# One order of pieces replaced by another in a fused Nyström attention and feed-forward kernel

## The chip, the core and the metric

The kernel runs on one core of a Trainium2 chip. The metric is the device time of one execution in microseconds (us). Before the change three runs took 248.09, 248.97 and 251.36 us, so the median is 248.97 us.

## The reference

Each of 8 batches has 8 heads, 576 positions and 64 columns a head. Queries and keys are averaged over 18 positions into 32 landmarks; three softmax matrices, an iterated inverse of the small one and the values give the attention's output, which goes through two dense layers with x * sigmoid(x) between them.

```python
q_lm = q.reshape(B, H, 32, 18, D).mean(axis=3)     # k_lm likewise
A  = sm(q, k_lm); Bm = sm(q_lm, k_lm); C = sm(q_lm, k)
Z  = Bm.T / (norm1(Bm) * norminf(Bm) + 1e-06)
for _ in range(6):
    Z = 2 * Z - Z @ Bm @ Z
x = A @ Z @ C @ v                                  # 4608 x 512
h = x @ w_in                                       # 512 x 2048
out = (h / (1 + exp(-h))) @ w_out                  # 2048 x 512
```

## The kernel before

The work is cut into some 1,500 named pieces. A piece is an object with a name, an engine, the pieces that it needs and a function that writes its instructions. The string SEQUENCE lists all names in one order; `Plan.run` walks it, gives each piece its PSUM banks (seven, and an eighth, bank 7, from the first piece of the second layer on) and its engine (`/ACT` or `/DVE` behind a name overrides the first choice), and the kernel writes the instructions in that order. Each engine then works through its own part of the list, in order, with semaphores where a piece needs another's data or buffer. No scheduler moves anything afterwards. A word `*n` stands for n fillers: matmuls of zeros into bank 7 that only keep TensorE busy.

Names used below, with the batch behind the dot and t = 1 for k, t = 0 for q, g for the half of the heads:

- `ld1.b`, `ld0.b`: load of k and q (GpSimd's queue, 576 KB each); `ldv0.b` to `ldv2.b`: the three loads of v (192 KB each); `wi..` and `wo..`: loads of the two weight matrices.
- `xt{t}{g}.b` (L539): DMA transpose of one half of k or q from the loaded tile `qk` to `qT`, issued on SyncE's queue, for batches 3 to 7. Batches 0 to 2 do this with TensorE pieces `tr..` and copies `trc..`.
- `lra`, `lrb`, `lrc`, `lrd{t}.b` (L575, VectorE): the sum over positions that makes the landmarks from `qT`; `ltr{t}.b` (TensorE) and `lmT{t}.b`: their transpose and its copy.
- `A.b`, `C.b`, `Ax..`, `Cx..`: the two large score matrices and their exponentials; `ct0.b`, `ct1.b` (L814): DMA transposes of the second one, on SyncE's queue, from batch 2 on; `cv.b`: the product with v.
- `ns..`, `nsd..`, `fb..`: the iterated inverse; `zt.b`, `m0.b` to `m3.b`: the product with the first weight matrix, two banks each, and their copies `mc{f}{g}.b` by ACT or VectorE.
- `h0.b` to `h15.b`, `hx0.b`, `hx8.b` (TensorE) and `g..`, `gx..` (ACT, L913 and L936): first layer and its activation; `h4` to `h7` read what `mc10` and `mc11` copied.
- `ss..@` (VectorE, L1001), `p1@` to `p7@` (TensorE) and `c..@`: the second layer as seven products of a block scheme; `os..@` (L978): four stores to the output, on SyncE's or ACT's queue.

Transfers wait for each other by hand. A piece's list `after` becomes a semaphore wait (L1126). Before the change it is fixed in code: `xt` of batch b and `ct` of batch b - 1 wait for `ldv1.b` (L534, L816), and the loads of batch b wait for the third transpose in the list of batch b - 1, which is `xt00`, and for `ct0` of batch b - 2 (L1096 to L1102). The list orders the transposes as xt10, xt11, xt00, xt01; SEQUENCE can issue them in another order.

## Time and profile before

| What | us |
|---|---|
| median of three runs | 248.97 |
| span of the profiled execution, first to last instruction | 245.4 |
| TensorE (PE) busy | 233.3 |
| ACT busy | 180.8 |
| VectorE (DVE) busy | 180.0 |
| weight loads (PEld), which overlap PE | 165.8 |
| GpSimd (POOL) busy, nearly all of it issuing loads | 36.7 |

The profile is of one execution. TensorE is busy in 95% of the span, in order, so the time is the sum of its pieces plus the waits between them. SyncE and GpSimd issue transfers; their rows show the issue, and a transfer lands later.

### The profile page before, as it was taken

The page shows a single profiled execution, that of the slowest core. Times are in us where ns is not written, and L with a number is a line of the kernel's source. Part 1 is how long each engine was busy: PE and PEld are TensorE (multiplying, and loading weights), DVE is VectorE, ACT ScalarE, POOL GpSimd, SP SyncE. Part 2 cuts the span into 40 slices and gives each one's busy share as a digit, 9 for nine tenths or more (in the row PEclk, how much of TensorE's full clock was granted, in tenths as well). Part 3 has the DMA queues.
Part 4 walks back from the last instruction along what each step waited for, and adds up shares of the span by engine and source line. Part 5 has one row for each costly group of instructions (what it writes and reads, how often), then busy time and mean ns, then how long its engine had stood idle before and what let it go on. Part 6 is the DMA issues. An engine that isn't in the chain of part 4 may idle for free.

```text
span 245.4 us, 7471 instructions
## 1 busy us (share of the span) xinstructions
PE 233.3 (95%) x2948; PEld 165.8 (68%) x2948; DVE 180.0 (73%) x503; ACT 180.8 (74%) x432; POOL 36.7 (15%) x62
## 2 busy tenths in 40 slices
PE   7999999999999999199999999999999999999992
PEld 5986464457867556067878754777876765789882
DVE  2589889789998591489798968938899475348752
ACT  3299999988989998159746699999779788634100
POOL 8346713000050040000130060000000000000000
PEclk9999999999999999769999999999999999999999
DMA  6999999999999999793999999985414421012343
GB/s 160 207 203 197 206 207 206 210 205 204 132 177 220 202 137 178 185 194 98 136 190 171 167 185 239 190 145 136 108 47 117 121 52 39 1 43 77 88 119 109
DMA packets 55876, 36.84 MB, mean 150 GB/s; under 512 B 36640, under 2 KB 47392, under 8 KB 55840
## 3 DMA queue, kind: packets, MB, share of 16 engines
q0 software_dynamic: 15120, 18.06, 45.1%
q1 hardware_dynamic: 39808, 17.35, 34.9%
q10 hardware_dynamic: 912, 0.95, 1.4%
q8 instruction: 23, 0.38, 0.6%
q14 instruction: 13, 0.11, 0.1%
HBM read 36.70 MB, written 9.44 MB: 188 GB/s over the span
## 4 chain that ended last, share of the span: by engine, by line
PE 78%; ACT 7%; DMA 7%; SPq 3%; issue 1%; DVE 1%; ACTq 0%; DVEq 0%
PE ps L325 74%; DMA qT<-qk 6%; PE ps L515 3%; SPq L539 2%; ACT gm L913 2%; DMA gm<-in_k_dram 1%; ACT L913 1%; SPq L814 1%; ACT L1116 1%; ACT gx L936 1%; ACT m L335 1%; PE ps L802 1%; DVE red L575 1%; ACT pb L641 1%; ACT et L742 0%
## 5 line engine op out<-in xcount | busy, mean ns | idle before, releaser
L913 ACT ACTIVATE gm<-ps 128x512 f16<-128x512 f32 x128 | 68.7, 621 | 15.0 <-PE ps L325 14.3
L325 PE MATMUL ps<-etn,m 128*128 128x512 bf16 (+1 forms) x512 | 73.5, 289 | 0.2
L325 PEld LDWEIGHTS <-gm 128*128 128x128 f16 x512 | 48.6, 98 | 12.5 <-issue 1.3
L325 PE MATMUL ps<-w_out_sb,gm 128*128 128x256 f16 (+1 forms) x392 | 53.0, 281 | 0.0
L325 PEld LDWEIGHTS <-ss 128*128 128x128 f16 x408 | 39.5, 99 | 9.8 <-issue 1.8
L325 PEld LDWEIGHTS <-m 128*128 128x128 bf16 x512 | 31.5, 98 | 20.8 <-issue 3.2
L325 PE MATMUL ps<-wt,ss 128*128 128x256 f16 x272 | 35.5, 276 | 0.2
L1036 DVE TENSOR_TENSOR ost<-ost,ps 128x256 f32<-128x256 f32 x51 | 20.9, 416 | 13.4 <-PE ps L325 7.4
L335 ACT COPY ost<-ps 128x256 f32<-128x256 f32 (+1 forms) x45 | 17.2, 388 | 10.9 <-PE ps L325 10.6
L335 ACT CAST m<-ps 128x512 bf16<-128x512 f32 x36 | 19.4, 612 | 1.1 <-PE ps L325 0.8
L337 DVE CAST m<-ps 128x512 bf16<-128x512 f32 x28 | 18.3, 685 | 2.3 <-PE ps L325 1.9
L710 DVE SCALAR_TENSOR_TENSOR st<-st,ps 128x128 bf16<-128x128 bf16 (+2 forms) x54 | 13.6, 257 | 8.5 <-PE ps L325 5.5
L407 POOL DMA_DIRECT2D v<-in_v_dram x24 | 14.0, 590 | 30.8 <-DMA qT<-qk 13.6
L325 PE MATMUL ps<-w_out_sb,ss 128*128 128x256 f16 x136 | 17.5, 273 | 0.0
L325 PE MATMUL ps<-wt,gm 128*128 128x256 f16 x120 | 15.5, 272 | 0.0
L575 DVE TENSOR_TENSOR red<-qT 128x1024 f16<-128x1024 bf16 x12 | 8.3, 689 | 9.4 <-DMA qT<-qk 9.2
L685 DVE TENSOR_TENSOR fb<-st,hmask 128x256 bf16<-128x256 bf16 (+1 forms) x54 | 14.4, 271 | 0.8
L752 ACT ACTIVATE ln<-ps 128x288 f32<-128x288 f32 x32 | 12.4, 423 | 2.7 <-PE ps L325 2.4
L787 ACT ACTIVATE ce<-ps 128x288 bf16<-128x288 f32 x32 | 13.0, 424 | 1.7 <-PE ps L325 1.6
L1001 DVE TENSOR_TENSOR ss<-gm 128x1024 f16<-128x1024 f16 x15 | 10.2, 686 | 5.2 <-ACT gm L913 5.2
L742 ACT ACTIVATE et<-ps 128x288 bf16<-128x288 f32 x32 | 11.1, 423 | 3.6 <-PE ps L325 3.6
L337 DVE COPY ost<-ps 128x256 f32<-128x256 f32 x25 | 10.5, 420 | 3.2 <-PE ps L325 3.0
(93 smaller groups left out, 332.0 us busy)
## 6 DMA issues: line engine op xcount, KB each, us to landing
out_dram<-ost SPq DMA_DIRECT2D x126, 64.0 KB, 2.1
v<-in_v_dram POOLq DMA_DIRECT2D x24, 192.0 KB, 10.0
qk<-in_q_dram POOLq DMA_DIRECT2D x7, 576.0 KB, 10.6
qk<-in_k_dram POOLq DMA_DIRECT2D x7, 576.0 KB, 9.2
w_out_sb<-in_moe_w_out_dram POOLq DMA_DIRECT2D x4, 512.0 KB, 15.1
w_in_sb<-in_moe_w_in_dram POOLq DMA_DIRECT2D x8, 128.0 KB, 7.2
w_in_sb<-in_moe_w_in_dram POOLq DMA_DIRECT2D x4, 256.0 KB, 9.0
out_dram<-ost ACTq DMA_DIRECT2D x10, 64.0 KB, 1.7
```

What stands on the lines that cost most here:

```text
L325: nc.tensor.matmul(out=out_ap, lhsT=lhsT, rhs=rhs, start=start, stop=stop, skip_group_check=True)
L335: nc.scalar.copy(out=out, in_=in_)
L337: nc.vector.tensor_copy(out=out, in_=in_)
L407: lambda e, a=a: nc.gpsimd.dma_start(out=v_r[b % 2][a * L:(a + 1) * L, :, :], in_=v[b].rearrange("h (l a x) d -> a l h (x d)", l=L, a=VA)[ ...
L575: lambda e: nc.vector.tensor_tensor(out=o_, in0=a_, in1=b_, op=OP.add),
L685: nc.vector.tensor_tensor(out=fb[it % 2][:, g0:g1], in0=bc(sr[it % 3][:, g0:g1, 0:L], 4, 2), in1=bc(hmask, n, 1), op=OP.mult), [o], 14.5 + ...
L710: nc.vector.scalar_tensor_tensor(out=s2[:, g0:g1, lo:SW], in0=s[:, g0:g1, lo:SW], scalar=2.0, in1=ps[:, 0:NG * SW].rearrange("p (g x) -> p ...
L742: lambda e, g=g, et=et, c=c: nc.scalar.activation(out=et[:, c], in_=bank(me["A"], 2 * g + c)[:, 0:HS], func=AF.Exp, scale=sc / J),
L752: lambda e, g=g, c=c, ln=ln: nc.scalar.activation(out=ln[:, c], in_=bank(me["S", g, c])[:, 0:HS], func=AF.Ln),
L787: nc.scalar.activation(out=ce[:, :, 0:VP].rearrange("p (i c) (a l) -> p c a i l", c=2, a=VA)[:, c], in_=bank(me["C"], 2 * g + c)[:, 0:HS]. ...
L913: lambda e, dc=dc, cell=cell: nc.scalar.activation(out=gm[:, dc, :], in_=bank(cell["o"]), func=AF.Silu),
L1036: nc.vector.tensor_tensor(out=out_, in0=x, in1=y, op=OP.add)
```

## The change

SEQUENCE is replaced as a whole: the same pieces, the same 2,948 matmuls and the same 64 fillers stand in another order. Of the copies and evacuations 86 go to the other of ACT and VectorE (43 each way), and 13 of the last stores to the other queue. Fillers also stand behind the point from which bank 7 is used by other pieces; before, all of them stood ahead of it. The waits in `after` are no longer made in code but written behind the name: `ldv1.5<xt00.4<ct0.3` waits for both. They follow the same rule as before (`xt` and `ct` wait for `ldv1`, loads for `xt00` and `ct0`), but each piece's place in the order is new. The helper that kept the list of GpSimd loads goes.

```diff
@@ Plan.run @@
+        placed = {}
...
+            word, *gates = word.split("<")
             name, _, e = word.partition("/")
             o = named.pop(name)
-            assert all(id(d) in seen for d, _ in o.deps), name
-            seen.add(id(o))
+            placed[name] = o
+            o.after = [placed[x] for x in gates]
@@ load @@
-    swdge = []
-    def load(name, prio, us, issue, emit, deps=(), after=()):
-        d = list(deps) + list(after)
-        if len(swdge) >= 8:
-            d.append((swdge[-8], None))
-        o = A(name, [("POOL", issue)], emit, d, prio, dma=us)
-        o.after = after
-        swdge.append(o)
-        return o
+    def load(name, prio, us, issue, emit, deps=(), after=()):
+        return A(name, [("POOL", issue)], emit, deps, prio, dma=us)
@@ attn @@
-                    qt_ops[t, g][0].after = gate
-                ct_ops[g][0].after = v_ops.get(b + 1, [])[-2:-1]
```

The order around the transposes of batch 4, by queue, taken from the two sequences:

```
SyncE before:  ct1.3 ct0.3 xt00.4 xt11.4 xt01.4 xt10.4 os@5020.0 os@5021.0 xt11.5 ...
SyncE after:   xt10.4 os@5021.0 ct0.3 os@5101.0 ct1.3 xt01.4 xt00.4 os@5020.0 xt11.4 xt11.5 ...
GpSimd before: ld1.4 ldv1.4 ld0.4 ldv0.3 ldv2.3 ldv2.4 | ld1.5 ldv0.4 ldv1.5 ld0.5 | ld0.6 ...
GpSimd after:  ld1.4 ldv2.3 ldv2.4 ldv1.4 ldv0.3 ld0.4 | ldv1.5 ld1.5 ldv0.4 ld0.5 ldv0.5 | ld1.6 ...
DVE before:    mc01.3 mc31.3 mc10.3 mc11.3 ss00@5200 ss00@5220 ss10@5200 lra1.4 lrb1.4 lrc1.4 ss10@5220 ss20@5220 lrd1.4
DVE after:     mc01.3 mc21.3 mc30.3 lra1.4 ss00@5200 ss20@5200 mc11.3 ss10@5200 lrb1.4 lrc1.4 lrd1.4
PE after:      m0.3 m2.3 m3.3 h6.2 h3.3 m1.3 h0.3 h13.3 *1 h15.3 h12.3 h8.3 p1@5200 h2.3 h10.3 h6.3 ... p6@5200 h11.3 ltr1.4
```

The bar in GpSimd's rows stands where the next load waits for transposes (`<xt00.4<ct0.3` for the second group).

The order of the weight loads is new too:

```
GpSimd before, behind ld1.1: ldv2.0 ldv0.0 wi0b1 ldv1.0 wi0b0 wi1a wi0a wi1b1 wi1b0 wi3b0 wi3a wi3b1 wi2b0 wi2b1 wi2a ldv0.1 ldv1.1
GpSimd after, behind ld1.1:  ldv1.0 ldv0.0 wi0a wi1b0 wi0b0 ldv2.0 wi3b1 wi1a wi1b1 wi3a wi3b0 wi0b1 wi2b1 wi2a wi2b0 ldv2.1 ldv0.1 ldv1.1
```

## The prediction

> **What bounds it now.** The page first: TensorE is busy nearly all the time, and one slice is not.

> ```profile
> PE 233.3 (95%) x2948; PEld 165.8 (68%) x2948; DVE 180.0 (73%) x503; ACT 180.8 (74%) x432; POOL 36.7 (15%) x62
> ...
> PE   7999999999999999199999999999999999999992
> ...
> PEclk9999999999999999769999999999999999999999
> ```

> The busy row has a single 1, near 100 us, and right behind it the granted clock falls to 7 and 6 tenths. The waits of TensorE say what that is, and the busy time by stretch what it costs.

> ```profile
> engine line waited for: us in total, times, longest us
> PE ps L325 <- DVE rs L575: 5.4, 1, 5.4
> PE ps L325 <- DVE zer L434: 1.1, 1, 1.1
> PE ps L325 <- ACT qk L335: 0.5, 1, 0.5
> PE ps L325 <- DMA ct<-ce: 0.2, 1, 0.2
> ```

> ```profile
> 95.00:98.75 3.75, 3.75 (x40) 2.66 (x37) 0.00 (x0) 3.75 (x9) 0.00 (x0) 1.00 1.21 199
> 98.75:104.17 5.42, 0.00 (x1) 0.00 (x1) 2.83 (x7) 0.44 (x1) 0.00 (x0) 0.76 0.74 182
> 104.17:110.00 5.83, 5.83 (x29) 3.54 (x30) 4.74 (x12) 2.75 (x7) 0.00 (x0) 0.64 1.04 197
> ```

> One wait of 5.42 us, then 5.83 us of matmuls at a clock of 0.64: they lose 5.83 x 0.36 = 2.1. So 7.5 us hang on one event. Everything else that TensorE waits for over 0.15 us is 1.8 us, 1.6 of it at the start. The chain of waits between 76 and 106 us, in start, length, what, and GpSimd's timeline show the event:

> ```profile
> 80.56 3.22 SPq L539
> ...
> 83.89 1.30 SPq L539
> ...
> 85.28 1.39 SPq L539
> ...
> 86.72 14.41 DMA qT<-qk
> ...
> 101.23 0.70 DVE red L575
> ```

> ```profile
> 86.34 0.71 POOL L400 DMA_DIRECT2D qk<-in_k_dram  x1 [13.68 <-issue]
> 87.04 1.16 POOL L407 DMA_DIRECT2D v<-in_v_dram  x2
> 88.20 0.71 POOL L400 DMA_DIRECT2D qk<-in_q_dram  x1
> ```

> The four transposes of batch 4 are issued as xt00, xt11, xt01, xt10. The loads of batch 5 wait for xt00 alone, the first: it lands at 85.81, and ld1.5 goes out at 86.34. xt01.4, issued 1.06 us ahead of that (85.28), lands in 3.8 us, as undisturbed ones do (3.3 to 4.2 for eight others). xt10.4, issued 0.38 behind it, takes 14.4: it lands at 101.14, the last of the four loads at 100.90. VectorE stands at lra1.4 meanwhile (8.0 us), and ltr1.4 on TensorE behind that. A transpose of qT is 1,152 packets of 256 bytes in the trace, a load of k or q 256 packets of 2,304, and while both are queued they take turns.

> [...]

> **The change, by part.** Durations below are of the trace, spacings from the starts of successive pieces on one engine (h 0.43, p 0.87, m 0.26, hx 0.47, ss 0.60, mc on VectorE 0.68, lra 0.69). TensorE's pieces are the same set, 222.2 us at these spacings, so only waits differ. Up to batch 3's first m both orders hold 80.3 us of pieces.

> *The transposes of batch 4.* SyncE now issues xt10, a store group, ct0.3, a store group, ct1.3, xt01, xt00, a store group, xt11; the loads wait for xt00, the third. The start is the landing of ldv1.4. ld1.4 keeps its place (66.9, landed 73.3); two v loads now stand ahead of ldv1.4, at 1.05 to 1.7 each, so it lands near 76.6 instead of 75.78. Then 1.38 (xt), 1.84 (four stores of 0.43 with gaps), 1.3 (ct), 1.84, 1.3, 1.38: xt00.4 goes out at T = 86.0 with gaps, and lands at T + 3.6. GpSimd needs another 0.55 after a landing (85.81 to 86.34, 66.33 to 66.90), so ldv1.5 goes out at T + 4.15 = 90.15. xt11.4 goes out behind xt00.4 and one store group, at T + 3.3 = 89.3: 0.85 ahead of the loads. Between the two rows, 1.06 ahead (clean) and 0.38 behind (held), it is nearer to clean: landing 92.9. Bounds of the lead: 0.4 (landing in 3.3, stores 0.3 slower) and 1.1.

> *What lra1.4 holds on VectorE.* Before, all four mc of batch 3 stood ahead of it; now lra1.4, ss00, ss20 and then mc11.3. mc11.3 is done 0.69 + 0.60 + 0.60 + 0.68 + 0.1 behind xt11.4's landing: 95.6. h6.3 reads it. From m0.3 to h6.3 stand four m, nine h, a p and a filler: 1.06 + 3.89 + 0.87 + 0.11 = 5.93, so without new waits h6.3 comes at 87.77 (batch 3's first m in the trace) + 5.93 = 93.7, with those below at 95.4. Wait: 0.2 (0 to 1.9). ltr1.4 stands 5.7 us of pieces behind h6.3 and its sums are done 1.6 behind mc11.3, so the old wait does not come back there.

> *The weights.* wi0b1 moves from third to twelfth behind ld1.1. All twelve weight loads and three v loads land by 29.05 in the trace, in a DMA that is full (share 1.19 and 1.25 from 10 to 30 us); behind wi0b1 now stand wi2b1, wi2a, wi2b0 (0.45, 1.24, 0.7 in the trace's landings), so it lands at 26.6. m0.0 would be due at 24.8 (0.9 earlier in the list than its 25.7). It waits 1.9, of which later waits before the change (the pieces there fall back by 1.0 to 30 us) are saved again; cv.1, now 4.8 us of pieces earlier, waits for ldv1.1 at about 32.1 and adds 0.3. Net 1.2, bounds 0 and 2.

> *ct1.3.* It goes out at 83.2 instead of 77.8 and lands 2.5 later (the shortest; 4.4 the longest): 85.8. cv.3 is due at 84.9. Cost 0.8 (0 to 2.7); the wait for ct that cv.3 has now, 0.2 and 0.2 around it, goes.

> *Fillers behind the use of bank 7.* Each must wait for that bank's evacuation: h9.1, filler 1.3 us later, behind g9.1 on ACT, which takes 0.62 and has a table load of 1.28 ahead. No row shows a filler so placed. Bounds 0 and 1.4 for the three; I take 0.2, since most stand over an ACT queue that was not behind before.

> *Engines of copies.* 43 against 43; per kind 9 more c (0.42), 7 fewer trc (0.46) and 2 fewer mc (0.68) on VectorE: within 1 us of 180 either way, cost 0 unless one sits ahead of a waited-for piece. Dropping the GpSimd bookkeeping writes no instruction: 0. Tail: one evacuation and stores behind the last p, as now: 0, within 0.3.

> Sum against the profiled execution: 245.4 - 7.5 - 0.4 + 0.2 + 1.2 + 0.8 + 0.2 = 239.9. The median of the runs stands 3.6 above the span, so 243.5.

> **Rivals.**

> *xt11.4 is caught.* It decides at the lead: if xt11.4 goes out later than the loads do (stores ahead of it held by 0.9 us), it waits for five loads. Price: 14.4 as in the trace, 1.26 for a fifth load: landing 105.0, mc11.3 at 107.7, h6.3 12.1 late, and 2.1 for the clock. 239.9 + 14.2 = 254.1, a time of 257.7: slower. For it: SyncE's store groups were held for 9.57 us behind a caught transpose. Against it: at 86 us no load is in flight. Chance 0.19. If only two fifths of its packets are left, it is held for ldv1.5 and most of ld1.5, 3.8 us: up to 249.4 with the clock, the forecast's upper end.

> The row for the clock is one wait of 5.42 us with 2.1 lost behind it; no row has a wait between 1.1 and 5.4. [...]

> *Many small waits.* The old order left slack around most pieces; here h6.3, cv.3, m0.0 and fillers all stand within 1 us of what they need, so ACT's and VectorE's queues may do the same at ten other places of 0.3 to 0.6 us (the trace has some 7 us of small ones between pieces, by how far starts fall behind the sum of spacings). + 4.5: 248. Chance 0.16.

> *Nothing new is late.* 245.4 - 7.9 = 237.5: 241.1. For it: a piece's wait vanishes when its producer is 1 us earlier. Chance 0.10.

> **The numbers.** Forecast 243.5, chance 0.55, its own range 240.5 to 249.5. 2% is 5.0 us, about what a measurement can tell from no change: faster means below 244.0, slower above 253.9. Faster: 0.41 of the forecast's 0.55 and 0.10 = 0.51. Slower: 0.19 and 0.03 from small waits and a half-caught transpose = 0.22. Within: 0.27. Range 240 to 254: it leaves out most of the caught case (0.17) and 0.03 below.

> **What would show it.** Right: no slice of TensorE under 8 near 100 us and no fall of the clock; the wait for rs L575 gone; xt11.4 issued just ahead of ldv1.5 and landed in under 5 us; small waits for w_in's load near 26 us and for ct near 85. Wrong: a wait of several us at an h for VectorE near 95 us (caught), or TensorE's short gaps together 4 us over those of before.

## The result and the profile after

The changed kernel takes 255.96 us (median of 5 runs, 254.70 to 258.75), the kernel before, in the same measurement, 250.15 us (248.09 to 251.36). The ratio is 1.027, with an interval of 1.021 to 1.034: 2.7% slower where 243.5 us was forecast. The ratio leaves out the executions of both kernels that ran in a slower state, and the profiled one of the changed kernel is of these: its span is 256.9 us, those of the other four are 252.8 to 255.2. The same two rows of the page as before, with the busy line:

```profile
PE 238.0 (93%) x2948; PEld 167.0 (65%) x2948; DVE 179.8 (70%) x503; ACT 182.7 (71%) x432; POOL 36.8 (14%) x62
...
PE   8989999989999859999839999999999999999993
...
PEclk9999999999999968999988999999999999999999
```

The 1 near 100 us is gone. In its place stand a 5 near 93 us and a 3 near 131 us, each with a lower clock in it or behind it, and the first half has 8s where there were 9s. TensorE's waits name the two:

```profile
engine line waited for: us in total, times, longest us
PE ps L333 <- DMA ct<-ce: 8.3, 3, 4.9
PE ps L333 <- ACT gm L910: 1.6, 2, 1.1
```

For VectorE's rs 0.5 us are left of 5.4. 8.3 us are waits for `ct`, which were 0.2. By stretch (busy time of each engine, then granted clock, DMA share, GB/s):

```profile
88.70:93.10 4.40, 1.00 (x50) 0.63 (x50) 0.00 (x0) 1.83 (x4) 0.00 (x0) 0.85 0.56 131
93.10:99.20 6.10, 6.10 (x50) 3.41 (x54) 2.51 (x7) 3.17 (x6) 2.55 (x4) 0.55 0.92 174
99.20:127.60 28.40, 28.40 (x335) 20.75 (x335) 24.72 (x66) 22.53 (x58) 1.34 (x3) 1.00 0.91 155
127.60:132.90 5.30, 0.42 (x40) 0.24 (x24) 2.28 (x7) 0.14 (x1) 0.00 (x0) 0.99 0.99 202
132.90:138.00 5.10, 5.10 (x67) 3.37 (x59) 1.30 (x5) 2.25 (x9) 1.87 (x3) 0.68 0.76 114
```

Two stalls, each followed by 5 to 6 us at a clock of 0.55 to 0.68. Between them TensorE works through 99 to 127 us without a gap, which is where the old stall would have been. The second stall in SyncE's and GpSimd's timelines (start, length, what):

```profile
120.24 1.21 SPq L812 DMA_TRANSPOSE ct<-ce  x1
121.55 2.97 SPq L975 DMA_DIRECT2D out_dram<-ost  x4
124.63 1.21 SPq L812 DMA_TRANSPOSE ct<-ce  x1
```

```profile
124.37 0.71 POOL L399 DMA_DIRECT2D qk<-in_k_dram  x1 [24.54 <-DMA ct<-ce]
```

The loads of batch 6 wait for `ct0.4`, the transpose at 120.24. It lands, ld1.6 goes out at 124.37, and `ct1.4`, held behind a store group, follows 0.26 us later. It lands at 132.54, 7.9 us after its issue; in the kernel before it took 4.4, and 2.5 is the shortest. This is the event that the prediction described for `xt10.4`, with another transpose.

To set kernels side by side, the table uses the measure of the prediction: by how much the starts of TensorE's pieces fall behind the sum of their spacings, in us, over stretches of that sum (222.2 us in all). What it contains are waits and matmuls at a lower clock.

| kernel | 0-40 | 40-75 | 75-88 | 88-95 | 95-110 | 110-222 | all | span |
|---|---|---|---|---|---|---|---|---|
| before | 6.2 | 0.8 | 0.7 | 7.6 | 0.7 | 2.7 | 18.6 | 245.4 |
| changed | 9.4 | 2.9 | 6.8 | 0.1 | 6.8 | 4.5 | 30.4 | 256.9 |
| changed, run again | 9.4 | 2.6 | 5.9 | 0.1 | 6.3 | 4.9 | 29.1 | 255.3 |

The old stall (88-95) is gone whole. What came instead is 3.2 us in the start, 1.8 to 2.1 up to 75, some 5 to 6 at `cv.3`, 6 at `cv.4`, and 2 spread over the second half. The differences of the spans (9.9 to 11.5 us) are larger than those of the medians (5.8, and 7.2 in the measurement of the repeated run), since the profiled execution of before is among its shortest, and the first one of the changed kernel its longest.

### The profile page after: what moved, and what is told of

It is laid out like the page before. It is cut to its first block, busy times and chain, and to the rows that moved or that the text cites. A ratio compares the mean times of both kernels' runs of the same rounds, so it can differ in the third digit from the quotient of the medians.

```text
span 256.9 us, 7465 instructions
## 1 busy us (share of the span) xinstructions
PE 238.0 (93%) x2948; PEld 167.0 (65%) x2948; DVE 179.8 (70%) x503; ACT 182.7 (71%) x432; POOL 36.8 (14%) x62
## 4 chain that ended last, share of the span: by engine, by line
PE 71%; DMA 11%; ACT 9%; DVE 3%; issue 2%; SPq 2%; POOL 1%; ACTq 0%; POOLq 0%; DVEq 0%
PE ps L333 69%; DMA qk<-in_q_dram 4%; DMA ct<-ce 4%; ACT gm L910 3%; DMA qT<-qk 2%; PE ps L514 1%; ACT L910 1%; ACT L1113 1%; SPq L538 1%; DVE red L573 1%; ACT m L343 1%; POOL qk L393 1%; ACT ln L750 1%; ACT pb L639 1%; DMA out_dram<-ost 1%
## 5 line engine op out<-in xcount | busy, mean ns | idle before, releaser
L910 ACT ACTIVATE gm<-ps 128x512 f16<-128x512 f32 x128 | 70.1, 648 | 15.4 <-PE ps L333 15.3
L333 PE MATMUL ps<-w_out_sb,gm 128*128 128x256 f16 (+1 forms) x392 | 55.3, 286 | 0.3 <-ACT ost L343 0.2
L333 PE MATMUL ps<-wt,ss 128*128 128x256 f16 x272 | 34.6, 273 | 0.0
L343 ACT COPY ost<-ps 128x256 f32<-128x256 f32 (+1 forms) x35 | 13.6, 404 | 20.3 <-PE ps L333 13.5
L343 ACT CAST m<-ps 128x512 bf16<-128x512 f32 x38 | 21.5, 617 | 2.5 <-PE ps L333 2.2
L345 DVE COPY ost<-ps 128x256 f32<-128x256 f32 x35 | 14.6, 420 | 9.7 <-PE ps L333 9.0
L345 DVE CAST m<-ps 128x512 bf16<-128x512 f32 x26 | 17.1, 685 | 3.6 <-PE ps L333 3.6
L333 PE MATMUL ps<-zer 128*128 128x256 bf16 x64 | 14.4, 328 | 2.7 <-DVE zer L433 1.1
L683 DVE TENSOR_TENSOR fb<-st,hmask 128x256 bf16<-128x256 bf16 (+1 forms) x54 | 14.4, 272 | 1.1
L998 DVE TENSOR_TENSOR ss<-gm 128x1024 f16<-128x1024 f16 x15 | 10.1, 686 | 5.8 <-ACT gm L910 5.8
L333 PEld LDWEIGHTS <-fb 128*128 128x128 bf16 x96 | 8.4, 99 | 7.1 <-DVE fb L683 2.5
```

The lines of the kernel that those rows point to most:

```text
L333: nc.tensor.matmul(out=out_ap, lhsT=lhsT, rhs=rhs, start=start, stop=stop, skip_group_check=True)
L343: nc.scalar.copy(out=out, in_=in_)
L345: nc.vector.tensor_copy(out=out, in_=in_)
L683: nc.vector.tensor_tensor(out=fb[it % 2][:, g0:g1], in0=bc(sr[it % 3][:, g0:g1, 0:L], 4, 2), in1=bc(hmask, n, 1), op=OP.mult), [o], 14.5 + ...
L910: lambda e, dc=dc, cell=cell: nc.scalar.activation(out=gm[:, dc, :], in_=bank(cell["o"]), func=AF.Silu),
L998: lambda e, o_=o_[:, k], x=x[:, k], y=y[:, k], op=op: nc.vector.tensor_tensor(out=o_, in0=x, in1=y, op=op), dep, 850.0 + prio / 100)
```

## Experiments

Theory A: transposes that go out too close to a load, or too late, carry the loss. Theory B: the loss is spread over many small waits, so that whatever is taken away, the next thing is late.

**The changed kernel again, and each `ct` alone.**

> The changed kernel once more, unaltered. Its first profile has 256.9 us of span, the longest of its five runs (the others 252.8 to 255.2), so the sizes of its waits may be too large. Theory A (two late transposes carry the loss): TensorE waits for ct twice, near 89 us (ct1.3, 3.9 us in two waits, some 6 us with the clock behind it) and near 128 us (ct1.4, 4.9 us), also in this run; these two together are 10 to 13 us. Theory B (the loss is spread over small waits, and one of the two ct waits is chance of that run): one of the two is under 1 us here, and the short gaps make most of the difference to before. Ratio to before 1.02 to 1.035.

257.12 us, ratio 1.031 (1.023 to 1.039). Both waits are there, 5.1 and 6.2 us with the clock (table; 75-80 and 105-110 of the sum): 11.3 together, as A has it. The next two runs issue one of them earlier each.

```diff
-SyncE: ct0.4 os@5201.0 ct1.4 os@5200.0
+SyncE: ct0.4 ct1.4 os@5201.0 os@5200.0
```

> The changed kernel with ct1.4 issued directly behind ct0.4, ahead of the store group os@5201.0 instead of behind it; nothing else moves. Theory A: ld1.6 still waits for ct0.4 alone and goes out some 3.8 us behind ct0.4's issue, so ct1.4 now leaves 2.5 us ahead of it instead of 0.3 behind, lands in under 5 us instead of 7.9, the wait of TensorE for ct near 128 us goes, and the kernel is 5 to 6.5 us faster than the changed one. Theory B: cv.4 is late for other reasons as well (its PE place or the load), at most 2 us are won.

252.83 us, ratio 1.013 (1.002 to 1.025), 4.3 us better than the repeated run. `ct1.4` left 4.25 us ahead of the load and landed in 4.2; the fall-behind at 105-110 went from 6.2 to 0.1 us. But 4.6 us came back at 110-120 where the repeated run has 1.6: ACT stood 3.1 us for a store group to land, which now goes out beside ld1.6, and TensorE waited for ACT. So A for the wait, with part of it given back; the profiled execution is the longest of four (two took 251.02), so that part need not be the same in each.

```diff
-SyncE: xt10.4 os@5021.0 ct0.3 os@5101.0 ct1.3 xt01.4
+SyncE: ct0.3 ct1.3 xt10.4 os@5021.0 os@5101.0 xt01.4
```

> The changed kernel with ct0.3 and ct1.3 issued ahead of xt10.4 and two store groups (still behind ldv1.4's landing); nothing else moves. Theory A: ct1.3 goes out some 6 us earlier and lands near 86 us, ahead of cv.3 (due near 88.7), so the wait for ct near 89 us and the fall of the clock behind it go: 5 to 6.5 us faster than the changed kernel. The transposes of batch 4 and the loads behind them keep their times within 0.5 us, as the same six things stand ahead of them. Theory B: cv.3 waits for something else then, at most 2 us are won.

252.94 us, ratio 1.014 (1.006 to 1.023), 4.2 us better. No wait for `ct` is left at all: `ct1.3` landed at 86.3, and `ct1.4`, by luck, left 0.89 us ahead of its load and landed in 2.5. Of the 11.3 us that went, 3.8 came back at once, at `h6.3`. The row of TensorE's waits, and the busy time by stretch around it:

```profile
PE ps L333 <- DVE m L345: 2.2, 1, 2.2
```

```profile
98.80:101.20 2.40, 0.25 (x2) 0.14 (x3) 2.37 (x5) 1.13 (x3) 0.64 (x2) 1.00 1.12 183
101.20:103.20 2.00, 2.00 (x15) 1.05 (x14) 1.90 (x6) 1.37 (x3) 0.00 (x0) 0.55 1.13 199
103.20:105.20 2.00, 2.00 (x21) 1.05 (x19) 1.93 (x7) 1.49 (x3) 0.00 (x0) 0.60 1.18 214
```

TensorE now comes to `h6.3` 5 us earlier and waits for mc11.3, which stands on VectorE behind lra1.4 and so behind `xt11.4`. That is the wait that the prediction sized at 0.2; a later TensorE had hidden it in the changed kernel.

**Is it the load, or the place behind the stores?** One semaphore, no instruction moved:

```diff
-ld1.6<xt00.5<ct0.4
+ld1.6<xt00.5<ct1.4
```

> The changed kernel with one wait exchanged: ld1.6 waits for ct1.4 instead of ct0.4. No instruction moves, ct1.4 still stands behind the store group. Theory A (the overlap with the load is what makes ct1.4 late): ct1.4 goes out near 124.4 as in the repeated run, lands in under 3.5 us instead of 5.9 to 7.9, and TensorE's wait for ct near 128 us shrinks from 3.8 to 4.9 to under 1.2 us: 3.5 to 5.5 us faster than the changed kernel, if the later load (some 3 us) is late for nobody. Theory B (ct1.4 is late because it stands behind the store group): the wait stays above 3 us and nothing is won.

253.13 us, ratio 1.016 (1.004 to 1.028). One wait for `ct` is left, that of `ct1.3`:

```profile
PE ps L333 <- DMA ct<-ce: 2.4, 1, 2.4
```

`ct1.4` went out at 123.56, again behind the store group, landed in 2.5 us, and TensorE did not wait (the fall-behind at 105-110 is 0.1). The load, 2 us later, was late for nobody: 110-125 costs 3.0 us, in the repeated run 2.4. So the overlap with the load is the cause (A), not the store group; the store group only makes the lead too short.

**Fillers.** The six fillers behind the first use of bank 7 are left out:

> The changed kernel without the six fillers that stand behind the first use of bank 7 (zero matmuls, so the output is the same). Theory A: a filler there waits for the evacuation of bank 7, and the two gaps at fillers (1.28 us near 54 us, 0.6 near 143 us) go and stay gone, with 0.7 us of filler work: 2 to 2.6 us faster than the changed kernel. Theory B: the piece behind each filler waits for the same ACT queue: under 1 us is won.

253.27 us, ratio 1.013 (1.002 to 1.024). The two gaps at fillers, 1.28 and 0.62 us, are gone; 0.4 of the first comes back soon behind it, at `h10.1`. Part of the 3.8 us against the repeated run has nothing to do with the fillers: `ct1.4` landed in 4.7 us instead of 5.9, and the fall-behind at 105-110 is 2.0 less.

**Taking one wait away after the other.** To the two `ct` edits comes lra1.4 behind mc11.3 on VectorE:

```diff
-DVE: mc30.3 lra1.4 ss00@5200 ss20@5200 mc11.3 ss10@5200
+DVE: mc30.3 ss00@5200 ss20@5200 mc11.3 lra1.4 ss10@5200
```

> The changed kernel with three edits together: ct0.3 and ct1.3 ahead of xt10.4, ct1.4 ahead of the store group, and on VectorE lra1.4 behind mc11.3 instead of ahead of ss00@5200 and ss20@5200. Theory A: both waits for ct go (6 and 5 us), and the wait of h6.3 for mc11.3 that showed up when the first was gone (2.2 us, 3.8 with the clock) goes too, because mc11.3 no longer stands behind the wait for xt11.4: 10 to 13 us faster than the changed kernel, 244 to 247 where the kernel before takes 250. The two transposes of batch 4 still need no more than 5.2 us each. Theory B: each wait removed is replaced by the next one (ACT behind stores that are held beside loads, 1.4 us near 133 us; VectorE near 103 us), and it stays within 2% of the kernel before.

252.44 us, ratio 1.011 (1.000 to 1.022): B. Both `ct` waits and that at `h6.3` are gone, and 5.3 us came at 95-100 of the sum. The chain of waits of this kernel shows by what (start, length, what):

```profile
106.05 2.84 SPq L538
...
110.49 1.71 DMA out_dram<-ost
...
112.32 0.44 DVE ost L345
...
112.80 5.26 PE ps L333 x43
```

TensorE waits for a copy on VectorE, that for its buffer, that for store group os@5100.0, which stands on SyncE behind two transposes of batch 5 whose issue is slow beside loads (2.84 us above; 1.28 and 1.37 for two of the changed kernel with no load beside them). So it was issued ahead of them:

```diff
-SyncE: xt11.5 xt10.5 os@5100.0 xt01.5
+SyncE: os@5100.0 xt11.5 xt10.5 xt01.5
```

> The changed kernel with the three edits of a_three, and the store group os@5100.0 issued ahead of xt11.5 instead of behind xt11.5 and xt10.5. In a_three TensorE waited 3.3 us near 112 us (5.3 with the clock) for a copy on VectorE, which waited 3.7 us for the landing of that store group at 112.2. Theory A (the store group stood on SyncE behind two transposes whose issue was slow beside loads): it now goes out near 101 to 104 us and lands by 108, and the 5.3 us go: 246 to 248 us where the kernel before takes 250 to 251, ratio 0.98 to 0.99. Theory B (VectorE is late there anyway, by xt11.5 for lra1.5): the wait stays with another name, ratio 1.00 to 1.01.

> As a_four, and without the six fillers behind the first use of bank 7. Theory A (waits for transfers that landed late, for stores behind them and for bank 7 are the whole loss against the forecast): a further 2 to 2.6 us, ratio 0.970 to 0.98, some 244 to 245 us, which is what was forecast for the change without them. Theory B (many small waits of the new order remain): 248 or more, ratio above 0.99.

With the fillers it takes 250.97 us (ratio 1.012, 1.004 to 1.019), without them 250.79 us (1.011, 1.004 to 1.019): B twice. The wait for the store is gone, but `xt11.5` now lands at 113.2 instead of 110.0, and four waits of 1.0 to 1.3 us (p6@5200, p2@5200, ltr0.5, sb.5) take its place (these numbers with the fillers), for sums and copies, most of them behind transposes of batch 5. The loads of batch 5 go out at 96.8 to 97.5, where the kernel before has 86.3, since their gate `xt00.4` lands 15.0 to 15.9 us behind ldv1.4 instead of 10.0. Between stand two store groups, and a third ahead of `xt11.4`.

```diff
-SyncE: ct0.3 ct1.3 xt10.4 os@5021.0 os@5101.0 xt01.4 xt00.4 os@5020.0 xt11.4 os@5100.0
+SyncE: ct0.3 ct1.3 xt10.4 xt01.4 xt00.4 xt11.4 os@5021.0 os@5101.0 os@5020.0 os@5100.0
```

> As a_five, and the four transposes of batch 4 issued one behind the other, ahead of the three store groups that stood between them; nothing else moves. In a_five the gate of the loads of batch 5 (xt00.4) landed at 96.2, 15.9 us behind ldv1.4, where in the kernel before it was 10 us, and the waits left behind 100 us are for the transposes of batch 5, 4.9 us in all (p6 at 104.7, ltr0.5 at 118, sb.5 at 120.7). Theory A (the store groups between the transposes hold the whole chain of loads up): the loads go out near 91.5 instead of 96.8, the transposes of batch 5 land some 4 us earlier, and 3 to 5 us are won: 246 to 248 us, ratio 0.98 to 0.992. Theory B (the waits there come from elsewhere, or the stores that go out later hold up ACT and VectorE): under 1 us is won, ratio 1.00 or more.

246.87 us, ratio 0.994 (0.989 to 0.998): 3.9 us won, A by the size, though the ratio is just above A's. The loads go out at 90.9, and the fall-behind at 95-110 goes from 3.2 to 0.2 us. A wait of 2.3 us at p6@5200 stays. The changed kernel with transfers alone mended (ct0.3, ct1.3 and the four transposes ahead of the store groups, and ld1.6 behind `ct1.4`), all compute instructions in place:

> The changed kernel with transfers alone mended: SyncE's order around batch 4 is ct0.3, ct1.3, the four transposes, then the store groups, and ld1.6 waits for ct1.4. No instruction of TensorE, ACT, VectorE or GpSimd moves, and the fillers stay. Theory A: both waits for ct go (10 to 12 us together with the clock), xt11.4 is early, so h6.3 does not wait, and the loads of batch 5 are 5 us earlier: 245 to 248 us where the kernel before takes 250 (ratio 0.98 to 0.992); what is left against the forecast of 243.5 is the start and the fillers, some 4 us. Theory B: new waits take more than half of it: ratio above 1.00.

249.03 us, ratio 1.003 (0.998 to 1.008): above A's 0.992 and at the edge of B, which began at 1.00. Mending transfers is worth 6 to 8 us against the changed kernel (1.027 and 1.031 in its two measurements), most of the loss.

**The old order with another gate.** One semaphore of the kernel before is exchanged; the loads of batch 5 wait for another of the four transposes, which go out as xt00, xt11, xt01, xt10:

```diff
 ld1.5 waits for:
-xt00.4
+xt10.4
```

> The kernel before with one wait exchanged: the loads of batch 5 wait for xt10.4, the last of the four transposes of batch 4 on the queue, instead of xt00.4, the first. No instruction moves. Theory A: xt10.4 is alone, lands in under 4 us (near 90.5 us), the wait of 5.4 us near 100 us and the fall of the clock are gone: 6.5 to 8 us faster than the kernel before (ratio 0.968 to 0.974). The loads go out some 4.5 us later and still land by 105 us. Theory B (something else is late right behind): the loads of batch 5 then come late for batch 5's transposes and products, and less than 3 us are won.

244.77 us, ratio 0.982 (0.975 to 0.990), between A and B; run again 245.74 us, 0.990 (0.985 to 0.994):

> The kernel before with the loads of batch 5 waiting for xt10.4, as run earlier, beside the kernel that waits for xt11.4. Ratio 0.975 to 0.99, 244 to 246 us. Theory A of the other kernel has this one 2 to 4.5 us slower than it, theory B 2 us or more faster.

The 7.6 us are gone, and 4.8 of them came back at 95-100: the loads go out at 92.8, 6.5 us later, so that VectorE stands 3.2 us at lra1.5 for a transpose of batch 5, with a piece behind it that TensorE needs. Moving the sums of batch 5 behind that piece:

```diff
-DVE: c12@5200 lra1.5 lrb1.5 lrc1.5 c22@5200 lrd1.5 c11@5200 pbs.4 pbr.4 bmx.4
+DVE: c12@5200 c22@5200 c11@5200 pbs.4 pbr.4 bmx.4 lra1.5 lrb1.5 lrc1.5 lrd1.5
```

> The kernel before with the exchanged wait (loads of batch 5 behind xt10.4) and, on VectorE, lra1.5 to lrd1.5 moved behind the second layer's c22, c11 and the three softmax steps pbs.4 to bmx.4. With the wait alone, VectorE stood 3.2 us at lra1.5 for a transpose of batch 5, c22@5200 behind it, and TensorE waited 2.9 us for that, 4.8 with the clock. Theory A: those 4.8 us go, 239 to 241 us where the kernel before takes 250 (ratio 0.955 to 0.965). Theory B: the sums of batch 5 are then late for ltr1.5, and the wait moves there: no better than with the wait alone (0.98).

246.32 us, ratio 0.988 (0.977 to 0.999): B. The 4.8 us went, and 2.6 came at ltr0.5 and 3.8 at cv.5. So this move on VectorE does not cure a late load. The gate in between:

```diff
 ld1.5 waits for:
-xt00.4
+xt11.4
```

> The kernel before with one wait exchanged: the loads of batch 5 wait for xt11.4, the second of the four transposes on the queue, instead of xt00.4, the first, or of xt10.4, the last, as in the earlier run. No instruction moves. Leads over the loads seen so far: 0.5 us and less landed in 5.2 to 14.4 us, 0.9 us and more in 2.5 to 5.0. Here xt11.4 lands near 88, the loads go out near 88.6, xt10.4 near 87.6, a lead of 1.0. Theory A (a transpose that is about 1 us ahead is clean): xt10.4 lands in under 6 us, the loads are out 4 us earlier than with the wait for the last one, and the new wait of 4.8 us that this brought (VectorE for a transpose of batch 5) falls under 1.5 us: 240 to 243 us where the kernel before takes 250, ratio 0.96 to 0.975. Theory B (only a transpose that has landed is safe): xt10.4 is held for over 8 us and the wait near 100 us is back, ratio 0.99 or more.

242.73 us, ratio 0.974 (0.969 to 0.979): A, and 2.6% faster than the kernel before, the fastest of all. Two rows of its page, and the longest of TensorE's waits:

```profile
PE   7999999999999999979999999999999999999992
...
PEclk9999999999999999999999999999999999999998
```

```profile
PE ps L325 <- DVE ost L1036: 1.2, 1, 1.2
```

`xt10.4` goes out 1.15 us ahead of the loads and lands in 4.6. No slice but the last has a clock under 9, and of the 4.8 us at 95-100 1.6 stay.

**The lead.** How long before the first load of the next batch a transpose goes out, and how long it takes to land. The last column says whether a packet on an instruction queue, of 16 KB, is in flight in that time. With neither a load nor an instruction packet beside it, `ct` takes 2.5 to 3.0 us and `xt` 3.2 to 3.6 in the sixteen traces.

| lead, us | transpose and kernel | landing, us | 16 KB packet |
|---|---|---|---|
| -0.38 | xt10.4, before | 14.4 | yes |
| -0.26 | ct1.4, changed | 7.9 | no |
| 0.25 | ct1.4, changed again | 5.9 | no |
| 0.32 | ct1.4, without fillers | 4.7 | no |
| 0.48 to 0.52 | xt11.4, changed (twice) and three more kernels | 5.2 to 6.6 | yes |
| 0.74, 0.75 | xt11.4, store ahead of xt11.5 | 5.2, 5.0 | no, one of 8 KB |
| 0.89 | ct1.4, ct1.3 early | 2.5 | no |
| 0.89, 1.22 | xt11.4, three edits; ct1.3 early | 3.2, 3.2 | no |
| 1.06 | xt01.4, before | 3.8 | yes |
| 1.15 | xt10.4, loads behind xt11.4 | 4.6 | yes |
| 1.6 to 1.9 | ct1.4, seven kernels | 2.5 (two), 4.2 to 5.2 (five) | no (two), yes (five) |

In the rows with "no" a lead of 0.32 us and less is held and one of 0.89 is not. In the rows with "yes" at 0.48 to 0.52 the load and the packet stand together, and no run parts them; from 1.06 us on a transpose is late only where the packet is there.

## Why the prediction was wrong

Its gain was right. The stall and its clock, 7.5 us in the forecast, are 7.6 in the table and went with the change. What it set against them was 2.4 us of new waits; the runs showed 18 to 19.

- *ct1.4: no term at all.* This is the step that failed. The prediction worked the race between a transpose and the loads out for `xt11.4` alone. The same order has `ct0.4`, a store group, `ct1.4`, and loads that wait for `ct0.4`; the gate was in the text, and the pair was not looked at. It cost 6.2 us in the repeated run, and 0.1 with the one semaphore exchanged.
- *ct1.3: 0.8 us (0 to 2.7).* The mechanism was right, the size was 5.1. Its wait was 3.7: ldv1.4 landed 0.9 later against TensorE than forecast, and SyncE took 8.3 us from there to `ct1.3` instead of 6.6, as `xt10.4` and a store group beside the last loads took 2.2 to 2.4 each. The other 1.4 is the clock, which the prediction gave to none of its waits.
- *The start: 1.2 us (0 to 2).* 2.5 us, above the bound: 0-40 is 9.4 in the middle of eleven traces with the new start (8.9 to 10.1) and 6.9 of five with the old one (6.2 to 7.6). The wait for w_in's load is only a part (0 to 0.7 from run to run). At tr114.0 and tr05.1 TensorE waits for the first loads of k and q (losing up to 1.7 and 1.0), and m1.0 for a copy on ACT (0.7).
- *Fillers: 0.2 us (0 to 1.4).* 1.9 us at two of them, 1.5 when what came back is taken off; above the bound either way. Six stand behind the first use of bank 7, not three. The cause was named; the filler behind h6.1 has the table load (1.28 us) ahead on ACT and paid 1.3.
- *h6.3: 0.2 us (0 to 1.9).* 0.5 in the repeated run, since `xt11.4` left 0.50 us ahead of the loads and not 0.85. Its 2.2 us to 3.8 with the clock appeared only when `ct1.3` no longer delayed TensorE.
- *Engines of copies, tail: 0.* No wait of these two showed up that an experiment tied to them.

The sum by the runs: 237.5 with nothing late (245.4 - 7.9), the transfers' 9.2 (255.3 less the 246.1 of the kernel with only its transfers mended), and 8.6 left over, which no run took apart further (the start, the fillers, the order of the compute pieces), makes 255.3. The rival "many small waits" had 4.5 of that on top of 2.4; it was true together with a caught transpose, and the two were forecast as alternatives. The caught rival's time, 257.7, came out near the measured one by luck, through `ct1.4` and `ct1.3`; `xt11.4` itself cost half a microsecond. The bridge from span to median, 3.6, was too large: within one execution the time is 1.9 above the span in the changed kernel's runs, and the rest is that the profiled execution of before was among its shortest.

That a transpose and a load take turns while both are queued is in the trace of before: from 97 to 99 us it has 158 packets of the transpose's queue and 158 of the loads'. The rows of `ct1.4` without a 16 KB packet fit that: it took 7.9 us at -0.26, 5.9 at 0.25, 4.7 at 0.32 and 2.5 at 0.89. That the forecast's own waits cost nothing at the clock was the author's estimate: no row of before showed a wait between 1.1 and 5.4 us. In the runs a wait of 2.2 us is followed by 0.55 and 0.60 in the rows above. So waits well under 5.4 us had to pay for the clock too.

What stays open: which of the small waits in the second half (4.9 us against 2.7) come from copies that changed engine. No run moved them back.

## What to carry to other kernels

When a new order is checked, list every transfer that goes out within about a microsecond of a load's gate, not the one pair that hurt in the old order; here 0.9 us ahead was clean and 0.3 was not. A gate on the last transpose kept it clear of the loads but started them late, and the next batch paid; of the three gates tried, the one in between, which still gave the last transpose 1.15 us of lead, was the best (0.974 against 0.982 and 0.990, and 1 for the first). A removed stall shows only what was hidden behind it, so compare by position how far the bound engine has fallen behind, and take the waits off in order of time.

## What the runs showed of the hardware that was not expected

The clock fell behind shorter waits than the 5.4 us seen before: to 0.55 behind 2.2 us above, to 0.52 behind 1.8 (loads behind xt10.4, sums moved), to 0.50 behind 1.1 and 1.3 close together (with fillers, store ahead of xt11.5), but not behind 2.3 at p6@5200 (four transposes together). The stretch behind the two short waits, and the wait of 2.3 with what follows it:

```profile
122.26:125.70 3.44, 3.44 (x20) 2.48 (x19) 0.58 (x3) 0.85 (x4) 0.71 (x1) 0.50 0.67 114
```

```profile
102.14:104.46 2.32, 0.01 (x2) 0.00 (x1) 0.48 (x2) 2.16 (x5) 0.00 (x0) 1.00 1.41 273
104.46:107.00 2.54, 2.52 (x20) 1.84 (x20) 2.47 (x7) 1.04 (x3) 0.00 (x0) 1.00 1.18 123
```

Some transposes took 1.5 to 2.4 us longer with no load under way: `ct0.4` of the repeated run 4.9 instead of 2.6. The queues between 119 and 124.1 us (packets, MB, share of 16 engines):

```profile
q1 hardware_dynamic: 971, 0.45, 36.3%
q8 instruction: 1, 0.02, 2.4%
q14 instruction: 1, 0.01, 0.6%
```

Beside SyncE's own queue these are two packets of instructions, the larger with 2.4% of 16 x 5.1 us, 2.0 us of transfer. Where `ct0.4` took 2.6 us (loads behind ct1.4), the large one came after its landing. The sixteen traces bear this out: 347 transposes had no load packet beside them, and 172 of these no instruction packet either; they landed in 2.5 to 3.0 us (`ct`) and 3.2 to 3.6 (`xt`). Every one of the 135 that took longer had an instruction packet in flight, up to 4.9 and 5.5 us. Another 40 had such a packet and took no longer. No run moved such a packet, so this stays an observation over all traces, not an experiment.
